# A second MLP in pairs of token blocks, with its weights reloaded for each pair and the output weights kept

## The chip, the cores and the metric

The kernel runs on one core of one Trainium2 chip. The metric is the time of one execution on the device in microseconds (us). Engines are named as the profile names them: PE multiplies matrices, PEld loads its stationary operand, DVE and ACT do elementwise work, SP issues DMA transfers. SBUF is the on-chip working memory, PSUM the accumulators that PE writes.

## The reference, cut to what matters

Attention in chunks of 64 tokens gives x, 4608 tokens by 512. Two MLPs follow; the second is the one that changes:

```python
def _moe_ref(x, w_in, w_out):               # d_ff = 2048
    h = x @ w_in
    g = np.maximum(h, 0.0) + np.log1p(np.exp(-np.abs(h)))
    return g @ w_out

def _moe2_ref(x, w1, w2, w3, w_out):        # d_model 512, d_ff = 768
    h = np.maximum(np.maximum(x @ w1, x @ w2), x @ w3)
    return h @ w_out
```

## The kernel before

Tokens go in nine blocks of 512 (`TB`). A value is carried as two float32r halves, a high and a low one, and a product is three matmuls (`PASS`: high by high, high by low, low by high). `cut_up` makes the halves: a cast (`copy_op`, ACT or DVE) and a subtraction (`tt_op`, DVE).

All work is first written down as operations for a planner (`Plan`). Each has the engines it may run on with a cost, its dependencies, the buffers it takes (`alloc`), a due time, and for transfers a landing time (`lat`, `move`). `Plan.order` walks through planned time and gives each engine the ready operation with the earliest due time whose buffers are free; the program is then written in that order, so the order on each engine, SP's queue included, and the place of each buffer are fixed before the run. PE's operations of the second MLP follow one another in the order written (`in_line("h", ...)`).

The large buffers are 46 slots of SBUF, each 128 partitions x 2 x 512 words (512 KB): kinds "w" (32), "x" (8), "z" (4), "qh" and "vh" (one each). Smaller ones are 13 tiles of 128 x 512 (kinds `LATE`) and three `g`. PSUM has two `ph` banks, two `acc` pairs of banks, and two banks `one` (X and Z), which hold sums that DVE adds up.

The second MLP multiplies by Strassen's scheme in Winograd's form: with both matrices in quarters, seven products (`SEVEN`, p1 to p7) in place of eight. Here the halves of X in the token direction are the two halves of one block, so `split` cuts a block into seven combinations (B11, T1 to T4, B21, B22), each one slot, and a product is 2 x 3 matmuls of 128 x 128 by 256 columns. The weights w1, w2, w3 are combined and cut once by `weights2` into nine units of 3 slots and a quarter tile shared by two units, which fill the "w" slots and stay for all nine blocks. A `Unit` is one block by one unit of weights: p1, p6, p2, p7 of the new unit are interleaved with p5, p4, p3 of the old one (`mlp2`). ACT copies products out of `ph` (`keep`), DVE adds those in `one` (`add`) and takes the maximum over w1, w2, w3. After every third unit two 128-row pieces of h are cut into `g`. `mlp2_out` is the output step: 12 matmuls of 512 columns with one 512 KB tile of w_out, loaded for that step from the cut copy in DRAM (`wo2d`) into one of two slots.

Before all that, attention and the first MLP run; `early` cuts w_out of the second MLP and converts w1 to w3 beside them, and the weights of the second MLP are cut as slots of the first one's weights come free.

The lines of the profile: 836 are the matmuls of a product, 954 those of an output step, 666 and 686 those of the first MLP, 254 and 256 the copies and casts, 261 DVE's combinations of two tensors, 939 the load of a w_out tile, 781 the load of X, 968 the store of the output.

Of the kernel before, what the change touches and what calls it, by code (L numbers as in the profile page):

```python
# [10 lines left out]
F32 = mybir.dt.float32  # L11
# [167 lines left out]
def tile_kernel(ctx: ExitStack, tc: tile.TileContext, q, k, v, w_in, w_out, w1, w2, w3, wo2, out):  # L179
# [22 lines left out]
    def mem(kind, n, shape, dt, where=pool):  # L202
# [14 lines left out]
        "pair": list(range(2)),  # L217
        "g": mem("g", 3, [P, 2, TB], F32R),
# [12 lines left out]
    w2d = [dram.tile([P, TB], F32, name=f"w2d{n}") for n in range(3 * NJ2)]  # L231
    x2d = [dram.tile([P, KD, TB], F32, name=f"x2d{b}") for b in range(NB)]

    names = [0]

    def slot(*kinds, shape=[P, 2, TB], dt=F32R):
        def fresh(i):
            names[0] += 1
            return pool.tile(shape, dt, tag=f"s{i}", name=f"s{i}_{names[0]}")

        return Buf(*kinds, fresh=fresh)
# [488 lines left out]
    LATE = ("tmp", "rq", "rk", "rv", "p")  # L730

# [14 lines left out]

    def weights2(n):
# [3 lines left out]
        pair = Buf("pair")  # L751
        for h, z in enumerate((a, b)):
            o = op(
                {"S": 0.48},
                lambda e, h=h, z=z: nc.sync.dma_start(out=z.t, in_=w2d[2 * n + h]),
                w=[z],
                alloc=[] if h else [a, b, c, d, pair, *ws[:3 if n % 2 else 4]],
                after=[store["w", 2 * n + h], *begun],
                lat=2.0,
                move=1.1,  # L760
            )
# [11 lines left out]
        return cut_up(ws[3], lambda: d.t[:, L], [d], cols=cols, key=n % 2, hold=[pair])  # L773

    def split(b, after):
        names = ("B11", "T1", "T2", "B21", "T3", "T4", "B22")
        raw = [slot("x", "z", dt=F32) for _ in range(2)]
# [16 lines left out]
        def make(name, one, two):  # L794
            view, t = src[name]
            z = x2[b, name] = slot("x", "z")
            tt_op(view, src[one][0], src[two][0], ALU.subtract, [src[one][1], src[two][1]], [t], alloc=[t, z])

        def put(name):
            made = (b, name) in x2  # L800
            z = x2[b, name] if made else slot("x", "z")
# [17 lines left out]

    clock = [T1]  # L820
# [6 lines left out]
    def product(b, n, p, dst, first, **kw):  # L827

        at, col, name = SEVEN[p]
        ws, x = wbuf["b", n][at], x2[b, name]  # L830
        col += HT * (n % 2) if at == 3 else 0
# [13 lines left out]
        return pe2(0.67, fn, r=parts_of(ws, n % 2 if at == 3 else "") + [x], **kw)  # L845

    class Unit:


        def __init__(u, b, n):  # L850
            u.b, u.n = b, n
            u.jp, u.i = divmod(n, 3)
            u.Y = Buf("ph")
            if u.i == 0:
# [16 lines left out]
        def y(u, p, **kw):  # L871
            return product(u.b, u.n, p, lambda: u.Y.t[:, :HT], p == 1, w=[u.Y], **kw)
# [22 lines left out]
        def p2(u):  # L895
            product(u.b, u.n, 2, lambda: two("X"), True, w=[(XZ, "X")], alloc=first_of(XZ))
            u.add(u.c[0], 0, "X")

        def p5(u):
            product(u.b, u.n, 5, lambda: two("Z"), True, w=[(XZ, "Z")])  # L900
# [5 lines left out]
        def p3(u):  # L906
            product(u.b, u.n, 3, lambda: two("Z"), False, w=[(XZ, "Z")])
# [3 lines left out]
            if u.i == 2:  # L911
                for f in range(2):
                    g = second[u.b, 2 * u.jp + f] = Buf("g")
                    cut_up(g, lambda f=f: u.m[f].t, [u.m[f]], alloc=[g])

# [11 lines left out]
    def two(key):  # L927
        return XZ.t["XZ".index(key)][:, :HT]
# [3 lines left out]

    def mlp2_out(b, j):
        g, wo = second[b, j], slot("qh", "vh")
        in_line(
            "wo2",
            op(
                {"S": 0.48},
                lambda e: nc.sync.dma_start(out=wo.t.bitcast(F32), in_=wo2d[j]),
                w=[wo],  # L940
                alloc=[wo],
# [3 lines left out]
            ),  # L945
        )
# [26 lines left out]
    def mlp2():  # L973

        units = [(b, n) for b in range(NB) for n in range(3 * NJ2 // 2)]
        old, outs = None, []
        for b, n in units + [(NB, 0)]:
            new = None
            if b < NB:
                new = Unit(b, n)  # L980
# [14 lines left out]
            if len(outs) > (b == NB - 1):  # L995
                mlp2_out(*outs.pop(0))
            if old and old.i == 2:
                outs += [(old.b, 2 * old.jp), (old.b, 2 * old.jp + 1)]
# [40 lines left out]
    split(0, begun)  # L1039
# [38 lines left out]
```

## Time and profile before

| | |
|---|---|
| median of 3 runs | 1455.72 us (1455.64 to 1456.2) |
| the profiled execution, its own time | 1458.03 us |
| its span, first to last instruction | 1456.2 us |
| PE busy | 1426.7 us, 98% of the span |
| DVE busy | 785.6 us, 54% |
| ACT busy | 454.2 us, 31% |
| DMA | 147.5 MB, 101 GB/s over the span |
| second MLP | about 890 us to the end; 61.80 us a block |

How to read it: busy time of PE is modelled and overlaps in a stream, so what a matmul costs is read from the chain of waits by time, where each piece starts as the one before ends. An idle time names what ended it. A transfer's time to landing runs from its issue on SP to its last byte.

### The profile page before, as it was taken

Reading aid. Unit: us, or ns where it says so; the run is one execution under the profiler, and the core shown is the slowest. Engines: PE = TensorE matmul, PEld = TensorE weight load, DVE = VectorE, ACT = ScalarE, POOL = GpSimd, SP = SyncE. Lnnn points to the kernel's source line nnn. Section 1 sums busy time; section 2 is a strip of 40 time slices with the busy share of each in tenths; the row PEclk is TensorE's granted clock in tenths of the full one; section 3 lists DMA queues with packets and bytes.
Section 4 is the critical chain, followed back from the end, with each engine's and each line's share of the span. In section 5 each row is a group of like instructions: output and inputs, shape, how many; then the busy total and the mean of one; then the engine's idle time right before and its main releaser. Section 6 shows DMA issues by size and latency. Waiting matters only on the chain.

```text
span 1456.2 us, 25977 instructions
## 1 busy us (share of the span) xinstructions
PE 1426.7 (98%) x10642; PEld 1242.4 (85%) x10642; DVE 785.6 (54%) x1551; ACT 454.2 (31%) x885; POOL 0.7 (0%) x7
## 2 busy tenths in 40 slices
PE   5999999999999999999999999999999999999998
PEld 4788888787888888888888888999999999999997
DVE  7887862655545544445443555555454644545443
ACT  4443332223223232232322444333232322323222
POOL 0000000000000000000000000000000000000000
PEclk8999999999999999999999999999999999999999
DMA  8563345655435334352231312132222322223122
GB/s 255 154 176 92 96 106 128 155 126 128 127 70 136 93 103 122 65 139 73 77 98 45 118 55 87 45 102 88 87 73 80 110 86 75 87 73 117 49 68 87
DMA packets 229079, 147.47 MB, mean 101 GB/s; under 512 B 168032, under 2 KB 196704, under 8 KB 228960
## 3 DMA queue, kind: packets, MB, share of 16 engines
q1 hardware_dynamic: 228144, 145.03, 34.7%
q8 instruction: 83, 1.36, 0.4%
q10 hardware_dynamic: 816, 0.79, 0.2%
q14 instruction: 36, 0.29, 0.1%
HBM read 109.58 MB, written 36.18 MB: 100 GB/s over the span
## 4 chain that ended last, share of the span: by engine, by line
PE 91%; DVE 3%; SPq 2%; DMA 2%; issue 1%; ACT 1%; ACTq 0%; DVEq 0%
PE acc L686 25%; PE ph L666 25%; PE ph L836 16%; PE one L836 12%; PE acc L954 10%; PE aps L471 2%; SPq L413 2%; DMA s<-in_moe_w_out_dram 1%; PE ph L374 1%; PE acc L471 0%; PE ph L375 0%; DVE tmp L261 0%; ACT s L254 0%; DMA s<-in_moe_w_in_dram 0%; DMA pd<-s 0%
## 5 line engine op out<-in xcount | busy, mean ns | idle before, releaser
L686 PE MATMUL acc<-g,s 128*128 128x512 f32 x1728 | 419.4, 391 | 5.0 <-DVE tmp L261 2.8
L666 PE MATMUL ph<-s,s 128*128 128x512 f32 x1728 | 416.9, 391 | 0.0
L686 PEld LDWEIGHTS acc<-g,s 128*128 128x128 f32 x1728 | 321.8, 188 | 73.5 <-issue 2.9
L666 PEld LDWEIGHTS ph<-s,s 128*128 128x128 f32 x1728 | 325.7, 189 | 68.2
L836 PE MATMUL ph<-s,s 128*128 128x256 f32 x1944 | 267.8, 283 | 0.0
L836 PEld LDWEIGHTS ph<-s,s 128*128 128x128 f32 x1944 | 251.8, 192 | 4.1
L261 DVE TENSOR_TENSOR tmp<-one,tmp 128x256 f32<-128x256 f32 x241 | 101.9, 423 | 246.9 <-PE one L836 217.4
L261 DVE TENSOR_TENSOR g<-tmp,g 128x512 fp32r<-128x512 f32 x198 | 135.5, 685 | 182.0 <-ACT g L254 181.6
L676 ACT ACTIVATE tmp<-ph 128x512 f32<-128x512 f32 x144 | 86.1, 598 | 450.1 <-PE ph L666 441.5
L254 ACT COPY tmp<-ph 128x256 f32<-128x256 f32 x268 | 100.0, 373 | 347.7 <-PE ph L836 346.5
L836 PE MATMUL one<-s,s 128*128 128x256 f32 x1458 | 201.6, 283 | 0.0
L836 PEld LDWEIGHTS one<-s,s 128*128 128x128 f32 x1458 | 186.7, 192 | 0.2
L954 PE MATMUL acc<-s,g 128*128 128x512 f32 x648 | 157.1, 391 | 0.5 <-DMA s<-wo2d 0.5
L954 PEld LDWEIGHTS acc<-s,g 128*128 128x128 f32 x648 | 118.3, 188 | 23.3 <-DMA s<-wo2d 0.9
L254 ACT CAST g<-tmp 128x512 fp32r<-128x512 f32 x196 | 121.8, 622 | 17.9 <-PE acc L686 8.4
L261 DVE TENSOR_TENSOR tmp<-tmp,tmp 128x256 f32<-128x256 f32 (+1 forms) x152 | 83.2, 548 | 4.0
L254 ACT CAST s<-tmp 128x512 fp32r<-128x512 f32 (+1 forms) x101 | 60.3, 602 | 41.1 <-DVE tmp L322 27.3
L595 DVE STREAM_TRANSPOSE s<-rq 128x512 f32<-128x512 f32 x28 | 19.9, 710 | 70.9 <-PE aps L471 43.9
L303 DVE TENSOR_SCALAR tmp<-s 128x512 int32<-128x512 int32 x56 | 23.6, 422 | 55.9 <-DMA s<-in_moe_w_dram 23.7
L261 DVE TENSOR_TENSOR s<-tmp,s 128x512 fp32r<-128x512 f32 (+1 forms) x72 | 46.3, 654 | 7.5 <-ACT s L254 6.7
L497 ACT ACTIVATE p<-p,drop 128x512 f32<-128x512 f32 x28 | 20.3, 725 | 66.4 <-DVE p L261 66.4
L254 ACT COPY tmp<-acc 128x512 f32<-128x512 f32 x53 | 29.9, 590 | 30.1 <-PE acc L954 15.8
(74 smaller groups left out, 669.9 us busy)
## 6 DMA issues: line engine op xcount, KB each, us to landing
s<-wo2d SPq DMA_DIRECT2D x54, 512.0 KB, 3.3
s<-in_moe_w_out_dram SPq DMA_DIRECT2D x22, 512.0 KB, 4.2
x2d<-tmp SPq DMA_DIRECT2D x36, 256.0 KB, 2.7
s<-in_moe_w_dram SPq DMA_DIRECT2D x18, 512.0 KB, 3.8
s<-x2d SPq DMA_DIRECT2D x18, 512.0 KB, 4.7
s<-in_moe_w_in_dram SPq DMA_DIRECT2D x16, 512.0 KB, 5.2
out_dram<-tmp SPq DMA_DIRECT2D x29, 256.0 KB, 4.5
pd<-s SPq DMA_DIRECT2D x28, 256.0 KB, 2.3
```

Source lines behind the costliest of these rows:

```text
L254: nc.scalar.copy(dst(), src())
L261: return op({"D": 0.69 * n}, lambda e: nc.vector.tensor_tensor(dst(), a(), b(), f), r=r, w=w, **kw)
L303: lambda e: nc.vector.tensor_scalar(ai(), hw(), 0x7FFFFFFF, None, ALU.bitwise_and),
L413: dma(out=dst().rearrange("p (g i) -> p g i", i=32)[a * 32:(a + 1) * 32, o // 32:(o + n) // 32, :], in_=src[b, t % HP * 2 + h, s:s + n, ha ...
L471: nc.tensor.matmul(dst[ROWS[k], r], w[ROWS[r]], x[ROWS[r]], start=True, stop=True)
L497: op({"A": 0.62}, lambda e: nc.scalar.activation(pbuf.t, pbuf.t, AF.Softplus, bias=drop[:, :1], scale=SCALE), w=[pbuf])
L595: op({"D": 0.69}, lambda e: nc.vector.transpose(qT(), Rq.t), r=[Rq], w=[(QK, "q")], alloc=[QK])
L666: nc.tensor.matmul(ph.t, w[:, wi, kk * P:(kk + 1) * P], x[kk].t[:, xi], start=(kk == 0 and wi == 0 and xi == 0), stop=(kk == KD - 1 and wi ...
L676: in_line("y", op({"A": 0.6}, lambda e: nc.scalar.activation(l.t, ph.t, AF.Softplus), r=[ph], w=[l], alloc=[l]))
L686: nc.tensor.matmul(acc[m // 2].t[:, m % 2], w[:, wi, m * P:(m + 1) * P], g.t[:, gi, :], start=(first and wi == 0 and gi == 0), stop=(last ...
L836: nc.tensor.matmul(dst(), ws.t[:, wi, col + kk * P:col + (kk + 1) * P], x.t[:, xi, kk * HT:(kk + 1) * HT], start=(first and kk == 0 and wi ...
L954: nc.tensor.matmul(acc[t // 2].t[:, t % 2], g.t[:, gi, t * P:(t + 1) * P], wo.t[:, wi], start=(j == 0 and wi == 0 and gi == 0), stop=(j == ...
```

## The change

Blocks are taken in pairs. The two halves of X in the token direction are now the two blocks of a pair, so each of the seven combinations is two slots of 512 columns (`split2`, 14 tiles, limited to 14 by the kind "xt"), and a product is 2 x 3 matmuls of 128 x 128 by 512 columns that fill a bank (`Unit2`). Four pairs go this way; the ninth block is left alone and goes through the old `Unit` and `split`.

X of a pair takes 14 slots and 6 for raw data, so the weights no longer fit beside it. Only unit 0 stays (`STAY = 1`). Units 1 to 8 are cut for the first pair as before, stored to DRAM (`w2c`, `w2e`), and read back for each later pair and for the ninth block (`again`). The kinds "ring" (3) and "ring1" (4) hold down how many units have weights in slots: three in the later pairs, up to seven in the first pair and the ninth block. Kinds "w" and "x" serve both purposes.

The six tiles of w_out are loaded once, into "qh", "vh" and "z", and stay. The h pieces of a pair's second block wait, in slots if need be, until the first block's output is done; up to two output steps follow one unit.

```diff
+        "ring": list(range(3)),
+        "ring1": list(range(4)),
+        "xt": list(range(14)),
...
+    STAY = 1
...
     def weights2(n):
-        ws = [slot("w") for _ in range(3)] + [wbuf["b", n - 1][3] if n % 2 else slot("w")]
+        ws = [slot("w", "x") for _ in range(3)] + [wbuf["b", n - 1][3] if n % 2 else slot("w", "x")]
...
+        ring = [Buf("ring", "ring1")] if n >= STAY else []
...
+        for k in range(3) if n >= STAY else ():
+            store["c", n, k] = op(
+                {"S": 0.48},
+                lambda e, k=k: nc.sync.dma_start(out=w2c[n][k], in_=ws[k].t.bitcast(F32)),
+                r=[ws[k]],
...
+        if n >= STAY and (n % 2 or n == 3 * NJ2 // 2 - 1):
+            w = slice(0, TB if n % 2 else HT)
+            store["e", n // 2] = op(
...
+    def again(n, *more):
+
+        if n < STAY:
+            return wbuf["b", n], []
+        ring = Buf("ring", *more)
+        ws = [slot("w", "x") for _ in range(3)] + [slot("w", "x") if n % 2 == 0 else wbuf["b", n - 1][3]]
+        new = ws[:3 if n % 2 else 4]
+        wbuf["b", n] = ws
+        for k, z in enumerate(new):
...
+                alloc=[] if k else [ring, *new],
+                after=[store["e", n // 2] if k == 3 else store["c", n, k]],
...
+        return ws, [ring]
...
+    def split2(two, after):
+
+        make = lambda: [slot("x", "w", dt=F32) for _ in range(2)]
+        R = make(), make()
+        T = make()
...
+        def put(name, v):
+            x2[two, name] = [slot("x", "w") for _ in range(2)]
+            held[two, name] = [Buf("xt") for _ in range(2)]
+            for kk, z in enumerate(x2[two, name]):
+                cut_up(z, lambda kk=kk: v[0][kk].t[:, v[1]], [(v[0][kk], v[1])], alloc=[z, held[two, name][kk]])
...
+    class Unit2:
...
+            u.ws, u.ring = (first_ws[n], rings[n]) if b[0] == 0 else again(n)
...
+                    for wi, xi in PASS:
+                        nc.tensor.matmul(
+                            dst(),
+                            ws.t[:, wi, col + kk * P:col + (kk + 1) * P],
+                            x[kk].t[:, xi],
...
+            return pe2(1.36, fn, r=[ws, *x], hold=u.ring + held[u.b, name], **kw)
...
     def mlp2_out(b, j):
-        g, wo = second[b, j], slot("qh", "vh")
-        in_line(
-            "wo2",
+        g = second[b, j]
+        if j not in wo2_of:
+            z = wo2_of[j] = slot("qh", "vh", "z")
             op(
...
     def mlp2():
 
-        units = [(b, n) for b in range(NB) for n in range(3 * NJ2 // 2)]
-        old, outs = None, []
-        for b, n in units + [(NB, 0)]:
+        groups = [(b, b + 1) for b in range(0, NB - 1, 2)] + [(NB - 1,)]
+        units = [(i, n) for i in range(len(groups)) for n in range(3 * NJ2 // 2)]
+        old, outs, side = None, [], []
+        for i, n in units + [(None, 0)]:
...
+                new = Unit2(groups[i], n) if i + 1 < len(groups) else Unit(NB - 1, n)
                 begin = new.p1()
-                if n == 1 and b + 1 < NB:
-                    split(b + 1, ready + [begin])
+                if n == 4 and i + 1 < len(groups):
...
-            if len(outs) > (b == NB - 1):
-                mlp2_out(*outs.pop(0))
+            for _ in range(2 if len(outs) > 3 else 1):
+                if len(outs) > (i is None or i + 1 == len(groups)):
+                    mlp2_out(*outs.pop(0))
```

The order of the instructions on PE is the same in both kernels up to the first product of the second MLP. From there on, in the regular part, it changes as follows. Rows of one kind that follow each other stand as one with a count; `ph` and `one` are the PSUM banks, `s` slots (the weights first, then X), `g` a piece of h, `acc` the output sums. Before, on PE, one unit's seven products and an output step:

```order
L836 MATMUL ph_89<-s_216_7276,s_237_7622 128x256 x6
L836 MATMUL one_7871<-s_217_7278,s_235_7546 128x256 x6
L836 MATMUL ph_90<-s_222_7343,s_235_7546 128x256 x6
L836 MATMUL ph_89<-s_220_7301,s_239_7624 128x256 x6
L836 MATMUL one_7871<-s_219_7299,s_233_7494 128x256 x6
L836 MATMUL one_7870<-s_218_7296,s_237_7622 128x256 x6
L836 MATMUL ph_89<-s_221_7323,s_239_7624 128x256 x6
L954 MATMUL acc_93<-s_214_7259,g_73 128x512 x6
L954 MATMUL acc_92<-s_214_7259,g_73 128x512 x6
```

After, on PE at the same kind of place, the last four products of such a row and the output step:

```order
L1042 MATMUL one_7917<-s_240_7597,s_262_8010 128x512 x3
L1042 MATMUL one_7917<-s_241_7602,s_262_8010 128x512 x3
L1042 MATMUL one_7916<-s_230_7480,s_263_8109 128x512 x3
L1042 MATMUL one_7916<-s_231_7499,s_263_8109 128x512 x3
L1042 MATMUL ph_90<-s_234_7537,s_265_8111 128x512 x3
L1042 MATMUL ph_90<-s_236_7558,s_265_8111 128x512 x3
L1148 MATMUL acc_93<-s_219_7299,g_72 128x512 x6
L1148 MATMUL acc_92<-s_219_7299,g_72 128x512 x6
```

A product has become two rows of three matmuls, one for each X tile, with twice the columns; the sequence of p1 to p7 and its interleaving of two units is the same. In all, 1512 matmuls of 512 columns and 378 of 256 stand where 3402 of 256 stood.

On SP, before, the last blocks' transfers are w_out tiles, X loads and output stores:

```order
L939 DMA s_372_12526<-wo2d_101 128x1024
L939 DMA s_373_12645<-wo2d_96 128x1024
L939 DMA s_374_12814<-wo2d_97 128x1024
L968 DMA out_dram<-tmp_83 128x512
L968 DMA out_dram<-tmp_82 128x512
L968 DMA out_dram<-tmp_81 128x512
L968 DMA out_dram<-tmp_80 128x512
L939 DMA s_375_12887<-wo2d_98 128x1024
```

After, on SP at the ninth block, the weights of its units come back (`w2c_0` to `w2c_2` are the three tiles of a unit, `w2e` the shared quarter tiles):

```order
L816 DMA s_447_10724<-w2c_0_123 128x1024
L816 DMA s_449_10726<-w2c_2_125 128x1024
L816 DMA s_448_10725<-w2c_1_124 128x1024
L816 DMA s_450_10798<-w2c_0_126 128x1024
L816 DMA s_454_10825<-w2c_0_129 128x1024
L816 DMA s_452_10800<-w2c_2_128 128x1024
L816 DMA s_451_10799<-w2c_1_127 128x1024
L816 DMA s_453_10801<-w2e_148 128x1024
L816 DMA s_457_10847<-w2c_0_132 128x1024
```

No w_out load is left there, and these nine are the first of 24 reloads that follow each other with no other transfer between them.

## Rows read from the trace of the kernel before

**Rows 1.** The page: span, PE's busy share, and the chain that ended last.

```profile
span 1456.2 us, 25977 instructions
PE 1426.7 (98%) x10642; PEld 1242.4 (85%) x10642; DVE 785.6 (54%) x1551; ACT 454.2 (31%) x885; POOL 0.7 (0%) x7
PE 91%; DVE 3%; SPq 2%; DMA 2%; issue 1%; ACT 1%; ACTq 0%; DVEq 0%
```

**Rows 2.** Busy time by stretch: first and last of seven regular blocks; columns as headed.

```profile
core 0: us, PE busy (x) PEld busy (x) DVE busy (x) ACT busy (x) POOL busy (x), PEclk, DMA share, GB/s
938.47:1000.27 61.80, 61.80 (x452) 58.86 (x451) 30.88 (x65) 19.00 (x45) 0.00 (x0) 1.00 0.26 86
...
1309.27:1371.07 61.80, 61.80 (x452) 58.85 (x451) 30.88 (x65) 19.00 (x45) 0.00 (x0) 1.00 0.26 86
```

**Rows 3.** The page's groups of matmuls: products and output steps.

```profile
L836 PE MATMUL ph<-s,s 128*128 128x256 f32 x1944 | 267.8, 283 | 0.0
...
L836 PE MATMUL one<-s,s 128*128 128x256 f32 x1458 | 201.6, 283 | 0.0
...
L954 PE MATMUL acc<-s,g 128*128 128x512 f32 x648 | 157.1, 391 | 0.5 <-DMA s<-wo2d 0.5
```

**Rows 4.** The chain by time (start, us, what): first MLP, then second MLP.

```profile
502.75 2.72 PE ph L666 x12
...
942.65 1.44 PE ph L836 x12
...
946.25 2.75 PE acc L954 x12
949.00 0.71 PE ph L836 x6
```

**Rows 5.** The end of the kernel: the chain by time, and DVE's last operation.

```profile
1442.94 2.76 PE acc L954 x12
...
1445.72 3.17 DMA s<-wo2d
...
1448.93 3.04 PE acc L954 x12
...
1444.89 0.69 DVE L261 TENSOR_TENSOR g<-tmp,g 128x512 fp32r<-128x512 f32 x1 [0.16 <-ACT g L254]
```

**Rows 6.** Transfers (KB each, us to landing), and the issue of a w_out load, ns.

```profile
s<-wo2d SPq DMA_DIRECT2D x54, 512.0 KB, 3.3
...
L939 SPq DMA_DIRECT2D s<-wo2d x24: 319/320/326, 1209.0 to 1445.7; - x24
```

**Rows 7.** DVE and ACT in one regular block, by form (count, busy, mean ns, idle).

```profile
L261 DVE TENSOR_TENSOR tmp<-one,tmp 128x256 f32<-128x256 f32 x27 | 11.4, 423 | 27.5 <-PE one L836 23.3 <-ACT tmp L254 4.2
L254 ACT COPY tmp<-ph 128x256 f32<-128x256 f32 x30 | 11.2, 373 | 39.2 <-PE ph L836 39.0
L261 DVE TENSOR_TENSOR tmp<-tmp,tmp 128x512 f32<-128x512 f32 x6 | 4.1, 691 | 0.2
L261 DVE TENSOR_TENSOR g<-tmp,g 128x512 fp32r<-128x512 f32 x6 | 4.1, 687 | 0.9 <-ACT g L254 0.9
L254 ACT CAST g<-tmp 128x512 fp32r<-128x512 f32 x6 | 3.7, 623 | 0.0
...
L261 DVE TENSOR_TENSOR tmp<-tmp,tmp 128x256 f32<-128x256 f32 x6 | 2.6, 425 | 0.2
L261 DVE TENSOR_TENSOR tmp<-ph,tmp 128x256 f32<-128x256 f32 x6 | 2.5, 417 | 0.0
...
L254 ACT COPY tmp<-acc 128x512 f32<-128x512 f32 x2 | 1.2, 586 | 1.8 <-PE acc L954 1.1 <-DVE tmp L256 0.7
```

**Rows 8.** Busy time by stretch again, columns as in rows 2: three stretches with dense transfers.

```profile
5.00:12.00 7.00, 4.87 (x99) 3.76 (x100) 6.43 (x14) 2.21 (x4) 0.00 (x0) 1.00 1.09 365
84.00:92.00 8.00, 8.00 (x37) 6.64 (x36) 8.00 (x18) 3.70 (x7) 0.00 (x0) 1.00 0.70 161
800.00:808.00 8.00, 8.00 (x37) 6.64 (x36) 2.33 (x4) 2.90 (x6) 0.00 (x0) 1.00 0.60 223
```

More of the change, by code (lines that the diff above doesn't have):

```diff
@@ L756, in weights2 @@
                 w=[z],
-                alloc=[] if h else [a, b, c, d, pair, *ws[:3 if n % 2 else 4]],
+                alloc=[] if h else [a, b, c, d, pair, *ring, *ws[:3 if n % 2 else 4]],
                 after=[store["w", 2 * n + h], *begun],
@@ L800, in put @@
             made = (b, name) in x2
-            z = x2[b, name] if made else slot("x", "z")
+            z = x2[b, name] if made else slot("x", "w")
             x2[b, name] = z
@@ L818, in split, with sub @@
         put("B22")
+    held = {}
+    def split2(two, after):
+        make = lambda: [slot("x", "w", dt=F32) for _ in range(2)]
+        R = make(), make()
+        T = make()
+        for h in range(2):
+            for kk in range(2):
+                for n, b in enumerate(two):
+                    op(
+                        {"S": 0.48},
+                        lambda e, h=h, kk=kk, n=n, b=b: nc.sync.dma_start(out=R[h][kk].t[:, n], in_=x2d[b][:, 2 * h + kk, :]),
+                        w=[(R[h][kk], n)],
+                        alloc=[] if n else [R[h][kk]],
+                        after=[store[b, 2 * h + kk]] + after,
+                        lat=2.0,
+                        move=1.1,
+                    )
+        def sub(z, a, b, alloc=False):
+            for kk in range(2):
+                view = lambda v, kk=kk: v[0][kk].t[:, v[1]]
+                tt_op(
+                    lambda view=view: view(z),
+                    lambda view=view: view(a),
+                    lambda view=view: view(b),
+                    ALU.subtract,
+                    [(a[0][kk], a[1]), (b[0][kk], b[1])],
+                    [(z[0][kk], z[1])],
+                    alloc=[z[0][kk]] if alloc else [],
+                )
+        def put(name, v):
[3 more added lines that the diff above has]
+                cut_up(z, lambda kk=kk: v[0][kk].t[:, v[1]], [(v[0][kk], v[1])], alloc=[z, held[two, name][kk]])
+        r11, r12, r21, r22, t1, t2 = (R[0], 0), (R[0], 1), (R[1], 0), (R[1], 1), (T, 0), (T, 1)
+        put("B11", r11)
+        sub(t1, r12, r11, True)
+        sub(t2, r22, t1)
+        put("T2", t2)
+        put("B21", r21)
+        sub(r12, r22, r12)
+        put("T3", r12)
+        put("T1", t1)
+        sub(r21, r21, t2)
+        put("T4", r21)
+        put("B22", r22)
     clock = [T1]
@@ L825, in pe2, with product @@
         return o
-    def product(b, n, p, dst, first, **kw):
+    def product(u, p, dst, first, **kw):
         at, col, name = SEVEN[p]
-        ws, x = wbuf["b", n][at], x2[b, name]
-        col += HT * (n % 2) if at == 3 else 0
+        ws, x = u.ws[at], x2[u.b, name]
+        col += HT * (u.n % 2) if at == 3 else 0
         def fn(e):
@@ L843, in fn @@
                     )
-        return pe2(0.67, fn, r=parts_of(ws, n % 2 if at == 3 else "") + [x], **kw)
+        return pe2(0.67, fn, r=[ws, x], hold=u.ring, **kw)
     class Unit:
@@ L853, in __init__ @@
             u.Y = Buf("ph")
+            u.ws, u.ring = again(n, "ring1")
             if u.i == 0:
@@ L906, in p3 @@
         def p3(u):
-            product(u.b, u.n, 3, lambda: two("Z"), False, w=[(XZ, "Z")])
+            product(u, 3, lambda: two("Z"), False, w=[(XZ, "Z")])
             u.add(u.c[0], 1, "Z")
```

135 lines of the change are left out of this document (114 added, 21 removed).

## The prediction

> **What bounds the kernel now.** I read the page first, then the stage table, then the chain of waits by time, then the operation groups. PE is busy for 98% of the span, and 91% of the chain that ended last is PE work [rows 1]. The chain's share is what counts: nearly every microsecond of the second MLP is a matmul waiting for the matmul before it. The stage table shows the regular part: each 512-token block of the second MLP takes 61.80 us, the same in the first regular block and in the last one, with PE busy throughout at a granted clock of 1.00, DVE busy 30.9 us, ACT 19.0 us and DMA a quarter [rows 2]. So only two things can shorten this stage: fewer or cheaper matmuls, or the removal of the one wait that shows, at the very end [rows 5]. The reader is to see in the page's groups that the second MLP's products (L836) are 1944 + 1458 = 3402 matmuls of 256 columns, 9 blocks of 378, and its output steps (L954) 648 matmuls of 512 columns [rows 3]. The mean durations there (283 and 391 ns) overlap their neighbours and are not prices. The price of a matmul in a stream is read from the chain by time, where each ends after the one before.
>
> **The products.** Twelve 256-column products in a row take 1.44 us, which is 120.0 ns each; twelve 512-column matmuls of the first MLP (L666), which read the same kind of slot and write a whole bank, take 2.72 us, 226.7 ns each [rows 4]. Two 256-column matmuls cost 240.0, one of 512 costs 226.7, so each pair that becomes one saves 13.3 ns. The change turns 8 of the 9 blocks into 4 pairs: 8 x 378 = 3024 small matmuls become 4 x 378 = 1512 wide ones; the ninth block keeps its 378 small ones. The order shows it: a product is now two runs of three 512-column matmuls where it was one run of six with 256. Saving: 1512 x 13.3 ns = **20.2 us**, all on the chain, since PE is the chain. The bound from the other side is the nearest 512-column row in this stage, the output steps: 2.75 us for twelve, 229.2 ns each [rows 4]. With that the saving is 1512 x 10.8 = 16.4 us. I take 226.7: the 2.75 stands beside a neighbour of 0.71 where half of its peers' 1.44 is 0.72, so part of the excess is only where the profile draws the border. If the excess is a price of changing between widths, most of the 48 output steps of the pairs lose it: a gain of at most 48 x 0.02 = 1.0 us more. I count it at nothing and keep it for the range.
>
> Beside it a rule speaks against so large a gain. The Trainium skill, "TensorE: Matmul & The Clock Gate", section Back-to-back issue gap, gives the gap of warm matmuls as the columns at 2.4 GHz plus 2.5 ns, so that width would hardly matter; the estimate by that page is 1512 x about 2.5 ns = 3.8 us instead of 20.2. The trace does not agree: at a granted clock of 1.00 [rows 2] the two rows, 120.0 and 226.7 ns, differ by 106.7 ns for 256 columns, and what is left over in each is 13.3 ns, not 2.5 [rows 4].
>
> **The w_out tiles.** Before, every output step loads its 512 KB tile again, 54 loads through two slots [rows 6]. After, six tiles are loaded once and stay. In the regular part these loads cost nothing (no wait for them stands in any regular block), so there is no gain there. At the end there is one: PE ends a step at 1445.70, waits 3.17 us for a w_out tile, and starts the last step at 1448.93 [rows 5]. The last operand from DVE was finished at 1444.89 + 0.69 = 1445.58, before PE came free at 1445.70, so nothing else is late behind the wait: **3.2 us** go. What follows (3.04 us of matmuls, the copy, the last stores) stays.
>
> **DVE and ACT.** The pair's work is re-cut, not enlarged. Before, one block costs DVE 39 operations of 256 columns (27 + 6 + 6, at 0.42 us) and 23 of 512 (6 + 6 and 11 for cutting X, at 0.69), 32.3 us, which is the stage table's 30.9 with the overlap [rows 2, 7]. After, a pair costs 51 combinations of 512 columns, 12 second halves of g and 24 operations for X: 87 x 0.69 = 60.0 us in a pair of about 118 us, where two blocks cost 64.6 in 123.6. The share stays at one half. ACT goes from 30 copies at 0.373 and 13 casts at 0.622 a block (19.3 us) to 30 copies at about 0.59 (the copy of 512 columns out of an accumulator) and 26 casts a pair: 33.9 us in 118 [rows 7]. A bank must be read within two products before PE needs it again; two products last 2.72 us now and lasted 1.44, and one operation of 512 columns takes 0.69, so the handover becomes looser. I cost all this at nothing. Its cover is the half of the time in which DVE is idle. Where it is thinnest is the change of pair, since the 14 X tiles of the next pair take the places of the old ones only as their last products end: 14 x 0.69 = 9.7 us of DVE inside some 20 us of PE work, beside the units' own work. If a quarter of that showed at each of the 3 changes it would cost 7 us; I keep 0 to 7 us for the range.
>
> **The reloads.** New work: in pairs 2 to 4 and for the ninth block, units 1 to 8 read their cut weights back, 3 tiles each and 4 more for the shared quarter tiles, one of them half: 27.5 loads of 512 KB, four times; and once the same is stored. Each costs SP about 0.32 us to issue and lands 3.3 us later when alone [rows 6]. 27.5 x 0.52 MB = 14.4 MB in a pair of 118 us is 122 GB/s, less the 54-load traffic that goes. The trace sustains 365 GB/s where the queue is kept full [rows 8]. Three sets are open: one finishing, one running, one loading; a set is freed in the middle of the next unit and refilled for a unit that begins about 15 us later, against 3.3 us and three more transfers at 1.44 us (0.52 MB at 365 GB/s), 7.6 us. So I cost the reloads at nothing in the pairs. SP's queue is in order: the reloads stand before the output stores and the X loads, whose consumers come a whole unit later. In the first pair, where weights are still cut by DVE, the 28.5 stores wait in SP for DVE; behind them stand loads of raw weights for units several places later, up to seven sets open.
>
> **The ninth block** is the tight place: its units of 42 x 120.0 ns = 5.04 us need 27.5 / 8 = 3.4 loads each, 4.9 us at 365 GB/s. What keeps it covered are the 14 output steps that the order puts into this stretch (14 x 2.72 = 38 us) and the reloads running up to seven sets ahead, as the order shows: 24 in a row on SP without a store between them.
>
> **Sum.** The profiled execution took 1458.0 us, 1456.2 of it span [rows 1]. 1458.0 - 20.2 - 3.2 = 1434.6 for a profiled execution; the median of the runs, 1455.7, lies 2.3 below it, so the forecast is **1432.3 us**.
>
> **Rivals.**
> *The ninth block waits for its weights.* For it: mixed stretches moved only 223 GB/s (800 to 808 us) and 161 (84 to 92) [rows 8]. At 223 a load takes 2.35 us and a unit's share 8.1 us, 3.0 more than a unit without output steps; two of the nine have none and four have two, so some 6 us stay: 1438. At 161 the 27.5 loads would take 90 us, more than the stage's own 83 us: some 1447. Against: a queue kept full held 365 for seven microseconds, and these reloads stand 24 in a row.
> *Columns, not matmuls, carry the cost.* If the wide products took twice 120.0 ns, only the 3.2 us would remain: 1455.7 - 3.2 = 1452.5. Against it stands the 226.7 of the first MLP. The page of the Trainium skill named above, TensorE: Matmul & The Clock Gate, would put it between, at an estimate of 1448.7.
> *Slower: the ring comes too late.* Place: the first product of each of the 32 reloaded units. If a set were freed a unit later than I think (its hold lasts until the last product of the unit, which runs inside the next), the landing would show, at least 3.3 us x 32 = 106 us: 1538. It decides from 23.4 / 32 = 0.73 us for each unit. For it: before, no weight moved at all in this stage, and nothing in the trace shows such a reload. Against: DMA busy only a quarter there [rows 2], and the 15 us against 7.6.
> *The change doesn't do what it says* is excluded by the order: 1512 wide and 378 small products stand in it.
>
> **How the numbers follow.** Forecast 0.77 (1430 to 1436: from 1.0 and 1.3 us below for the output steps and the runs' own spread, to 3.8 above for 229.2 ns); small waits at the changes of pair 0.05 (1434 to 1440); ninth block 0.10 (1436 to 1441); columns 0.03; ring 0.05. The range 1429.5 to 1440 holds the first two and most of the third, about 0.88, and is no wider than these bounds. A measurement here tells 0.2%, 2.9 us, from no change. Faster: all but the ring and half of the columns, 0.93; within 0.2%: 0.02; slower: 0.05.
>
> **What would show it.** Right: twelve 512-column products in 2.72 us in the chain by time, a pair in about 118.3 us (378 x 0.2267 + 12 x 2.72), no idle of PE before the pair's products (line 1042 of the changed kernel), the last step starting as the one before ends, DVE near one half. Wrong: "DMA s<-w2c" or "s<-w2e" in the chain (ring, or ninth block by its place), DVE or ACT as releaser of PE at the change of pair, or 2.88 us for twelve wide products (columns).

## The result, and the profile after

The changed kernel takes **1433.43 us** (median of 4 runs, 1432.72 to 1436.79) where the kernel before took 1455.96 beside it (4 runs, 1455.64 to 1457.31). The ratio is **0.9848**, 95% interval 0.9831 to 0.9865: 22 us less, between 19.7 and 24.6. The forecast was 1432.3 in a range of 1429.5 to 1440. The whole comes out right and one of its two terms does not, as the runs below show.

The page of the kernel after, against [rows 1] and [rows 3]: its span, the engines' busy time, the chain that ended last by engine, and the matmul groups of the second MLP. Products of the pairs are now line 1042, those of the ninth block line 942 (not in the table's largest groups), output steps line 1148.

```profile
span 1430.9 us, 22911 instructions
...
PE 1406.5 (98%) x9130; PEld 1164.8 (81%) x9130; DVE 769.3 (54%) x1400; ACT 437.3 (31%) x760; POOL 0.7 (0%) x7
...
PE 94%; SPq 2%; DMA 2%; DVE 1%; issue 1%; ACT 1%; ACTq 0%; DVEq 0%
...
L1042 PE MATMUL ph<-s,s 128*128 128x512 f32 x864 | 212.3, 389 | 0.0
...
L1042 PE MATMUL one<-s,s 128*128 128x512 f32 x648 | 158.8, 389 | 0.0
...
L1148 PE MATMUL acc<-s,g 128*128 128x512 f32 x324 | 77.6, 390 | 0.0
L1148 PE MATMUL acc<-s,s 128*128 128x512 f32 x324 | 77.3, 389 | 0.0
```

There are 864 + 648 = 1512 wide products, as forecast, and the idle time before every one of these groups is 0.0. The 0.5 us that stood before the output steps in [rows 3] is gone. PE is still the chain.

The chain by time (start us, us, what), first in a pair, then at the end of the kernel:

```profile
1010.89 2.72 PE ph L1042 x12
1013.61 2.72 PE one L1042 x12
1016.33 1.36 PE ph L1042 x6
1017.69 5.44 PE acc L1148 x24
...
1413.28 2.75 PE acc L1148 x12
1416.03 0.71 PE one L942 x6
1416.74 0.72 PE ph L942 x6
1417.46 0.85 PE one L942 x6
1418.31 8.20 PE acc L1148 x36
```

Twelve wide products take 2.72 us, 226.7 ns each, the price that the prediction took from the first MLP. Twenty-four output matmuls between them take 5.44, also 226.7 each; in the ninth block, between products of 256 columns, twelve take 2.75 again. At the end, the last three output steps run as one piece of 36: the wait of [rows 5] is gone.

Busy time by stretch (columns as in [rows 2]): one pair from a place in it to the same place in the next, then the first two stretches of 20 us behind the ninth block's first product, which starts at 1338.48.

```profile
1121.05:1239.37 118.32, 118.32 (x523) 97.99 (x523) 57.87 (x91) 34.03 (x59) 0.00 (x0) 1.00 0.43 158
...
1340.00:1360.00 20.00, 20.00 (x134) 18.43 (x133) 9.33 (x18) 5.74 (x13) 0.00 (x0) 1.00 1.02 402
1360.00:1380.00 20.00, 20.00 (x126) 18.09 (x126) 5.58 (x12) 3.28 (x8) 0.00 (x0) 1.00 0.30 105
```

A pair takes 118.32 us (forecast 118.3), against 2 x 61.80 of two blocks in [rows 2]; DVE is busy 57.87 us of it (forecast 60.0) and ACT 34.03 (33.9), PE the whole. From 1340 to 1360, while the ninth block's weights come back, the DMA engines are full, share 1.02 and 402 GB/s, more than the 365 that the prediction had seen in [rows 8], and PE is busy in every one of those microseconds.

For all that follows, **the stage** is the time from the first product of the second MLP to the end of the last matmul, both from the chain by time. What comes before it is the same work on PE in both kernels.

| kernel | first product, us | last matmul ends, us | stage, us |
|---|---|---|---|
| before | 889.36 | 1451.97 | 562.61 |
| after | 885.77 | 1426.51 | 540.74 |

The stage is 21.87 us shorter. Its pieces of the chain, added up by line: products 407.83 before (3402 matmuls, 119.9 ns each), 388.17 after (1512 at 226.7 and 378 at 120.1), 19.7 less; output steps 229.6 ns for each matmul before and 227.1 after, 1.6 less over 648; and 0.5 of a wait at the end. (The front ended 3.6 us earlier in this one execution; the last experiment shows that it moves by as much from run to run.)

### The profile page after: what moved, and what is told of

The parts are those of the page before. It is cut to its first block, busy times and chain, and to the rows that moved or that the text cites. A ratio compares the mean times of both kernels' runs of the same rounds, so it can differ in the third digit from the quotient of the medians.

```text
span 1430.9 us, 22911 instructions
## 1 busy us (share of the span) xinstructions
PE 1406.5 (98%) x9130; PEld 1164.8 (81%) x9130; DVE 769.3 (54%) x1400; ACT 437.3 (31%) x760; POOL 0.7 (0%) x7
## 4 chain that ended last, share of the span: by engine, by line
PE 94%; SPq 2%; DMA 2%; DVE 1%; issue 1%; ACT 1%; ACTq 0%; DVEq 0%
PE acc L691 26%; PE ph L671 26%; PE ph L1042 14%; PE acc L1148 10%; PE one L1042 10%; PE aps L476 2%; PE ph L942 2%; PE one L942 1%; SPq L418 1%; PE acc L476 1%; PE ph L379 1%; DMA s<-in_moe_w_out_dram 1%; ACT s L259 1%; PE ph L380 0%; DMA s<-in_k_dram 0%
## 5 line engine op out<-in xcount | busy, mean ns | idle before, releaser
L671 PE MATMUL ph<-s,s 128*128 128x512 f32 x1728 | 416.8, 391 | 0.1
L671 PEld LDWEIGHTS ph<-s,s 128*128 128x128 f32 x1728 | 325.6, 189 | 68.2 <-DVE s L266 0.2
L1042 PE MATMUL ph<-s,s 128*128 128x512 f32 x864 | 212.3, 389 | 0.0
L266 DVE TENSOR_TENSOR tmp<-one,tmp 128x512 f32<-128x512 f32 (+1 forms) x125 | 79.1, 633 | 213.8 <-PE one L1042 175.4
L1042 PEld LDWEIGHTS ph<-s,s 128*128 128x128 f32 x864 | 162.2, 188 | 33.6
L259 ACT COPY tmp<-ph 128x512 f32<-128x512 f32 (+1 forms) x140 | 75.8, 542 | 278.4 <-PE ph L1042 218.1
L1042 PE MATMUL one<-s,s 128*128 128x512 f32 x648 | 158.8, 389 | 0.0
L1042 PEld LDWEIGHTS one<-s,s 128*128 128x128 f32 x648 | 121.5, 188 | 25.1
L1148 PE MATMUL acc<-s,g 128*128 128x512 f32 x324 | 77.6, 390 | 0.0
L1148 PE MATMUL acc<-s,s 128*128 128x512 f32 x324 | 77.3, 389 | 0.0
L1148 PEld LDWEIGHTS acc<-s,s 128*128 128x128 f32 x324 | 60.6, 188 | 12.5
L266 DVE TENSOR_TENSOR tmp<-tmp,tmp 128x512 f32<-128x512 f32 (+1 forms) x112 | 69.4, 621 | 2.4
```

Source lines behind the costliest of these rows:

```text
L259: nc.scalar.copy(dst(), src())
L266: return op({"D": 0.69 * n}, lambda e: nc.vector.tensor_tensor(dst(), a(), b(), f), r=r, w=w, **kw)
L671: nc.tensor.matmul(ph.t, w[:, wi, kk * P:(kk + 1) * P], x[kk].t[:, xi], start=(kk == 0 and wi == 0 and xi == 0), stop=(kk == KD - 1 and wi ...
L1042: nc.tensor.matmul(dst(), ws.t[:, wi, col + kk * P:col + (kk + 1) * P], x[kk].t[:, xi], start=(first and kk == 0 and wi == 0 and xi == 0), ...
L1148: nc.tensor.matmul(acc[t // 2].t[:, t % 2], g.t[:, gi, t * P:(t + 1) * P], wo.t[:, wi], start=(j == 0 and wi == 0 and gi == 0), stop=(j == ...
```

## The experiments

In the edited kernels the lines shift a little: products of the pairs are 1042 or 1044, output steps 1148 or 1149. Line 1134 is the load of a w_out tile, 816 the reload of weights, 886 the load of X for a pair, 259 a copy on ACT.

### Width alone

**e1_halves** keeps the whole change, pairs, reloads, resident w_out, and splits each wide product matmul back into two of 256 columns.

```diff
-                for kk in range(2):
-                    for wi, xi in PASS:
-                        nc.tensor.matmul(
-                            dst(),
...
-                            x[kk].t[:, xi],
-                            start=(first and kk == 0 and wi == 0 and xi == 0),
+                for c in range(2):
+                    part = slice(c * TB // 2, (c + 1) * TB // 2)
+                    for kk in range(2):
+                        for wi, xi in PASS:
+                            nc.tensor.matmul(
+                                dst()[:, part],
...
+                                x[kk].t[:, xi, part],
+                                start=(first and c == 0 and kk == 0 and wi == 0 and xi == 0),
...
```

> The changed kernel with each 512-column product matmul of the pairs split into two of 256 columns; reloads, resident w_out, DVE and ACT work stay. Theory (a matmul carries a fixed 13.3 ns beside its columns): 3024 matmuls of 120.0 ns instead of 1512 of 226.7, so 20.2 us longer: about 1453.6 us against 1433.4. The stretch from the first product to the last matmul, 540.7 us in the changed kernel, becomes about 561. Rival (the gain comes from the fewer and longer DVE and ACT operations or from the resident w_out, not from the width): stays within 3 us of 1433.4. The page TensorE: Matmul & The Clock Gate of the Trainium skill would give an estimate of 3.8 us longer.

Measured: 1456.22 us (10 runs), ratio to before 0.9998 (0.9989 to 1.0008); stage 561.46, which is 20.72 longer than after's, as expected. The median is 2.6 above the expected 1453.6; in the one execution with a profile the first product starts at 889.12, 3.35 later than in after's, so that the excess lies ahead of the stage. Its chain by time, near the place shown above of after:

```profile
1017.59 1.43 PE ph L1044 x12
1019.02 1.44 PE one L1044 x12
1020.46 2.88 PE ph L1044 x24
```

120.0 ns each, exactly [rows 4]. So nearly all of the gain hangs on the width of the product matmuls: pairs, the ring and the resident tiles with narrow products give no gain that the medians can tell. (Twice the columns also means half as many matmuls and half as many weight loads; no run parts these.) The stage is 1.15 us shorter than before's; 0.53 of that is the wait at the end. Most of the rest lies in the output steps: added up matmul by matmul in PE's trace, with the waits left out, they take 148.6 us before, 147.8 here and 147.1 after. So half of what they gain is there without the width, and the other half came with it. Here and in the kernel after they stand in 36 runs between products, before in 52; whether that brings the first half is not shown.

**e2_quarters** goes one step on, four matmuls of 128 columns (`range(4)` and `TB // 4` in the same edit), to ask whether 13.3 ns is a fixed price for each matmul whatever its width.

> The same with four matmuls of 128 columns: a third width for the price law. Theory (13.3 ns fixed plus 0.4167 ns a column, from 120.0 and 226.7): 66.7 ns each, 6048 of them 403 us instead of 343, so about 1494 us. Rival (each matmul loads its own weights, and that load sets a floor near the 120 ns seen at 256 columns): 6048 x 120 = 726 us, so about 1816 us. In between means a floor between 66.7 and 120 ns.

Measured: 1769.97 us (one run), stage 875.14. The chain by time:

```profile
1014.92 5.36 PE one L1044 x48
1020.28 5.36 PE ph L1044 x48
```

5.36 / 48 = 111.7 ns each, not the 66.7 of a straight line through 120.0 and 226.7. Halving the columns from 256 to 128 saves 8 ns instead of 53. The line through 256 and 512 columns does not reach down to 128. It looks like a floor near 111 ns, lower than the 120 of the rival, but no narrower width was run. The Trainium skill, "TensorE: Matmul & The Clock Gate", section LDWEIGHTS, gives the time of a weight load as its columns at 1.2 GHz; by that the estimate for the 128 columns that each matmul here loads is 106.7 ns, and the 111.7 is 5 ns above it. It fits, but no run here changed the weight load, so that cause is not shown. The Trainium skill's section Back-to-back issue gap, on the same page, does not fit: its sustained 81 ns for 128 columns and 131 for 512 stand against 111.7 and 226.7.

### The w_out tiles

**e4_before_wo_ahead** puts the one gain that the prediction saw in w_out, 3.2 us, into the kernel before: in the last block the six tiles get slots of their own, those that X no longer needs, and so arrive early.

```diff
-        g, wo = second[b, j], slot("qh", "vh")
+        g, wo = second[b, j], slot("qh", "vh", "z") if b == NB - 1 else slot("qh", "vh")
```

> The kernel before, with four more slots for the w_out tiles of the last block alone, so that they are loaded ahead: the resident w_out's effect at the end, alone. Theory (0.5 us of idle PE): the stretch from the first product to the last matmul shrinks from 562.6 to about 562.1 us; the time is the same within its noise, 1455.4. Rival (3.2 us, as predicted): 559.4 us, and 1452.8.

Measured: 1455.61 us (10 runs), ratio 0.9994 (0.9983 to 1.0005); stage 561.78, 0.83 shorter than before's. PE has no wait left in the stage, and what went with it is far from 3.2 us. Why, PE's timeline of the kernel before shows (start us, us, engine, line, operation, count, and in brackets the idle time ahead of it and what ended it):

```profile
1442.78 5.63 PE L954 MATMUL acc<-s,g 128*128 128x512 f32 x24
1448.93 3.02 PE L954 MATMUL acc<-s,g 128*128 128x512 f32 x12 [0.53 <-DMA s<-wo2d]
```

From 1442.78 PE ran two steps, 24 matmuls, and not one; it was idle for 0.53 us. The chain of [rows 5] follows the load back to its issue at 1445.72 and leaves out the second of the two steps, which ran beside the transfer. The page's row had the right number all along, 0.5 us in [rows 3].

**e3_wo_again** takes the resident tiles out of the kernel after: w_out is loaded again for each output step, as before.

```diff
-        if j not in wo2_of:
-            z = wo2_of[j] = slot("qh", "vh", "z")
+        wo = slot("qh", "vh")
+        in_line(
+            "wo2",
...
-                lambda e: nc.sync.dma_start(out=z.t.bitcast(F32), in_=wo2d[j]),
+                lambda e: nc.sync.dma_start(out=wo.t.bitcast(F32), in_=wo2d[j]),
...
```

> The changed kernel with w_out loaded again for every output step through two slots, as before the change; all else stays. Theory (the wait at the end of the kernel before was only 0.5 us of idle PE, the rest of the 3.17 us on the chain lay beside an output step): 0.5 us longer at the end, 1434. Some 2 to 3 us more are possible in the ninth block, where these loads now queue behind the reloads on SP; they would show there as PE waiting for a w_out tile. Rival (the wait was worth 3.2 us at the end, as predicted): 1436.6, with 3.2 us of idle PE before the last step.

Measured: 1442.61 us (4 runs), ratio 0.9909 (0.9894 to 0.9924); stage 547.93, 7.2 longer than after's, when 0.5 was expected and 3.5 at most. PE's waits in the stage (engine, line, for what: us in total, times, longest):

```profile
PE ph L1042 <- ACT tmp L259: 3.0, 2, 2.2
PE acc L1149 <- DMA s<-wo2d: 2.7, 3, 1.4
```

Only 0.5 of this is the wait at the end; the 1.5 of the 7.2 that are no wait lie in the matmuls right behind the five waits. ACT, the other releaser, was itself held (its timeline, then the waits of SP's queue in the stage, here and in the kernel before):

```profile
1063.44 0.59 ACT L259 COPY tmp<-ph 128x512 f32<-128x512 f32 x1 [6.33 <-DMA out_dram<-tmp]
```

```profile
SPq L1134 <- PE acc L1149: 334.7, 51, 19.9
...
SPq L939 <- PE acc L954: 490.1, 52, 17.7
```

SP stood 334.7 us before w_out loads whose slot PE had not yet left. In such a time nothing behind goes out: not the output stores, whose `tmp` ACT needs for its next copy, and not the reloads. The kernel before has the same wait, 490.1 us of it in the stage, and PE waited there for nothing but the 0.53 us at the end; it had no reloads to stand behind. Both waits for ACT stand in the sixth of a pair's nine units, in pairs 2 and 3, soon after SP has loaded X for the next pair. In the ninth block it goes the other way round, the reloads stand ahead of w_out (busy time by stretch, columns as above):

```profile
1370.00:1380.00 10.00, 9.13 (x61) 8.24 (x60) 3.93 (x8) 2.15 (x5) 0.00 (x0) 1.00 1.02 414
1380.00:1390.00 10.00, 8.61 (x56) 7.56 (x55) 0.85 (x2) 1.12 (x3) 0.00 (x0) 1.00 0.49 168
```

That this is the queue's order and not the transfers was so far a reading. **e8_wo_pool** tests it: e3_wo_again with the w_out loads issued from GpSimd's queue, which has nothing else to do there. PE's order stays.

```diff
-                {"S": 0.48},
-                lambda e: nc.sync.dma_start(out=wo.t.bitcast(F32), in_=wo2d[j]),
+                {"G": 0.48},
+                lambda e: nc.gpsimd.dma_start(out=wo.t.bitcast(F32), in_=wo2d[j]),
```

> The kernel with w_out loaded again for each output step (e3_wo_again), with one thing changed: those 54 loads are issued from GpSimd's queue, which is otherwise empty there, and no longer from SP's. PE's order of work is the same. Theory (SP's queue is in order, so a w_out load that waits for its slot holds the stores and reloads behind it, and the prefetched reloads hold the w_out loads): the second MLP's waits of PE for ACT (3.0 us) and those for w_out in the ninth block (2.2 us) vanish; only the wait before the last step, about 0.5 us, may stay. The stage (first product of the second MLP to the last matmul's end) takes 540.7 to 541.5 us and not 547.9; the median about 1434 to 1436 us. Rival (the transfers themselves: the w_out loads take the DMA engines' time from the reloads, or come late by their own 3 to 9 us of landing): the stage stays at 545 to 548 us, median 1440 to 1443.

Measured: 1436.03 us (4 runs), ratio 0.9863 (0.9847 to 0.988); stage 542.32. The same bytes move, and 5.6 of the 7.2 us are back; the stage is 0.8 above the top of what the theory gave. GpSimd's waits, then PE's timeline at the only wait that PE has left in the stage:

```profile
POOL s L1134 <- PE acc L1149: 603.3, 52, 146.5
```

```profile
1420.04 5.63 PE L1149 MATMUL acc<-s,g 128*128 128x512 f32 x24
1426.92 3.01 PE L1149 MATMUL acc<-s,g 128*128 128x512 f32 x12 [1.25 <-DMA s<-wo2d]
```

GpSimd waits 603.3 us for the slots and PE loses nothing by it; no other transfer of the stage is issued there. The waits for ACT and those inside the ninth block are gone, as the theory said; the last one is 1.25 us and not 0.5, since that load goes out 0.4 us later than from SP and takes 3.52 us from issue to landing where [rows 5] has 3.17. What e8_wo_pool does not part is a load that is issued late and one that lands late behind reloads issued before it: in e3_wo_again the w_out load that ended the 1.39 us wait in the ninth block went out at 1373.20, once SP had issued the reloads ahead of it, and then took 9.34 us to land. The Trainium skill has the place of the wait for GpSimd's path: by "DMA: Bandwidth & Descriptors", section Anatomy of one DMA — SWDGE (gpsimd) path, DMA engines do not wait on semaphores, the issuing sequencer does, before it dispatches. GpSimd's 603.3 us agree, and so do the 334.7 of SP's queue.

### The ring and the ninth block

**e5_ring2** gives the ring of the reloads two sets instead of three (`"ring": list(range(2))`); the borrowed slots of `ring1`, by which sets run further ahead, stay.

> The changed kernel with two sets of reloaded weights open in the later pairs instead of three (six instead of seven in the first pair and the ninth block): the ring brought one step nearer to the rival that it comes too late. A unit's reload can then start only when the last product of the unit before it has run, some 4 us of products and one or two output steps (2.7 to 5.4 us) before its own first product. Theory (a reload takes 3.3 us for its first tile and 1.4 for each more, and the tiles are needed one after another over the unit): just enough, no PE wait, 1433 to 1435 us, stage 540.7 to 542. Rival (the ring is near its edge): 24 units wait 1 to 3 us each, 1457 to 1505.

Measured: 1433.84 us (4 runs), ratio 0.9851 (0.9835 to 0.9868); stage 540.73 and no wait of PE in it. One set fewer costs nothing, so the rival (24 units wait) falls.

**e7_two_sets** takes the borrowed slots too, so that the reloads of the ninth block can run one unit ahead and not seven.

```diff
-        "ring": list(range(3)),
+        "ring": list(range(2)),
...
-            u.ws, u.ring = again(n, "ring1")
+            u.ws, u.ring = again(n)
```

> As the run with two sets, and two sets in the ninth block too (before: six). There the units last 5.04 us without an output step, and a unit's 3.4 reloads take 4.9 us at 365 GB/s. Theory (the sets loaded ahead are what covers the ninth block): 3 to 10 us of PE waiting for w2c or w2e tiles in the last 90 us, none in the pairs; 1436 to 1444. Rival (transfers are far from the bound there): stage 540.7, no waits, 1433.4.

Measured: 1435.2 us (4 runs, 1434.56 to 1436.61), ratio 0.9859 (0.9845 to 0.9874); stage 540.74, no wait of PE. The expected 3 to 10 us do not show. The stretches of the table above, in this kernel:

```profile
1340.00:1360.00 20.00, 20.00 (x129) 18.22 (x128) 8.40 (x16) 5.79 (x13) 0.00 (x0) 1.00 0.09 36
1360.00:1380.00 20.00, 20.00 (x126) 18.09 (x125) 6.09 (x13) 3.13 (x8) 0.00 (x0) 1.00 0.74 280
```

The same transfers lie later, 36 and 280 GB/s where after has 402 and 105, and still in time. Of the two covers that the prediction named for the ninth block, the reloads far ahead are not needed, as long as no w_out load stands in SP's queue; the other, the output steps between its products, is still there and was not tested.

**e9_both_small** takes that last condition away: w_out again through SP (e3_wo_again) and two sets (e7_two_sets) together.

> The kernel with w_out loaded again for each output step (e3_wo_again), with the shorter ring for the reloads (two sets and no borrowed slots, as in e7_two_sets). What it tells apart: whether the wait of the ninth block comes from the 24 reloads that stand ahead of the w_out loads on SP. Theory: with two sets hardly any stand ahead, so the 2.2 us of waits for w_out in the ninth block vanish, while PE's waits for ACT at the start of pairs (3.0 us), where w_out loads hold the stores, stay: stage about 545 to 546 us, median about 1438 to 1440. Rival (the w_out loads wait for their own slots, whatever stands ahead): no change from e3_wo_again, stage 547 to 548.5 us; or, if now the reloads come late behind waiting w_out loads, longer, up to 555 us.

Measured: 1456.23 us (10 runs), ratio 0.9998 (0.9986 to 1.001); stage 566.91, 26.2 longer than after's. Alone the one costs 7.2 us and the other nothing; together they eat the whole gain. Neither expectation reached that far. PE's waits in the stage:

```profile
PE ph L942 <- DMA s<-w2c: 8.2, 5, 3.0
PE ph L1042 <- DMA s<-w2c: 7.2, 3, 3.1
PE ph L942 <- ACT tmp L259: 0.5, 1, 0.5
PE acc L1149 <- DMA s<-wo2d: 0.5, 1, 0.5
```

The theory was right that the w_out waits of the ninth block go (0.5 is the end's), and wrong that the pairs keep their waits for ACT. Now a w_out load that waits stands ahead of a reload that is needed at once. In the pairs this is not at their start, where the expectation had put the waits for ACT: all three waits stand in the sixth of nine units, in pairs 2, 3 and 4. SP's timeline ahead of the first of them:

```profile
1040.22 1.30 SPq L886 DMA_DIRECT2D s<-x2d  x2
1049.72 0.32 SPq L1134 DMA_DIRECT2D s<-wo2d  x1
...
1052.44 0.32 SPq L1134 DMA_DIRECT2D s<-wo2d  x1
1052.81 0.91 SPq L816 DMA_DIRECT2D s<-w2c  x2
```

For 8 us, up to 1049.72, nothing goes out, since a w_out load waits for its slot; the reload that PE needs goes out at 1052.81, behind the next w_out load. The other five waits for reloads are in the ninth block.

All waits together are 16.4 us. In the other 9.8 PE waits for nothing. Where such time goes the matmuls right after a wait show (PE's timeline, then busy time by stretch, columns as above):

```profile
1059.26 2.90 PE L1042 MATMUL ph<-s,s 128*128 128x512 f32 x6 [2.77 <-DMA s<-w2c]
...
1182.31 2.90 PE L1042 MATMUL ph<-s,s 128*128 128x512 f32 x6 [3.06 <-DMA s<-w2c]
...
1305.20 1.61 PE L1042 MATMUL ph<-s,s 128*128 128x512 f32 x6 [1.40 <-DMA s<-w2c]
...
1411.31 0.95 PE L942 MATMUL ph<-s,s 128*128 128x256 f32 x6 [2.32 <-DMA s<-w2c]
...
1415.95 0.95 PE L942 MATMUL ph<-s,s 128*128 128x256 f32 x6 [2.26 <-DMA s<-w2c]
```

```profile
1059.26:1062.15 2.89, 2.89 (x7) 2.31 (x8) 0.36 (x1) 0.00 (x0) 0.00 (x0) 0.50 1.05 408
...
1064.00:1066.00 2.00, 2.00 (x11) 1.64 (x10) 1.90 (x4) 0.00 (x0) 0.00 (x0) 1.00 1.00 399
1182.31:1185.21 2.90, 2.90 (x7) 2.32 (x8) 0.07 (x1) 0.00 (x0) 0.00 (x0) 0.50 1.05 410
...
1305.20:1308.00 2.80, 2.79 (x12) 2.34 (x13) 0.00 (x0) 0.59 (x1) 0.00 (x0) 1.00 0.96 345
...
1411.31:1413.60 2.29, 2.29 (x18) 2.18 (x18) 0.48 (x2) 0.37 (x1) 0.00 (x0) 1.00 0.98 381
...
1417.30:1420.50 3.20, 3.20 (x17) 3.20 (x17) 1.54 (x3) 0.06 (x2) 0.00 (x0) 0.50 1.03 421
```

After 2.77 us without work the granted clock is 0.50, the lower of the two levels (1.2 GHz), and six wide matmuls take 2.90 us, more than twice their usual 1.36; soon after it is 1.00 again. After 3.06 it is the same; after 1.40 it stays at 1.00, and the six take 1.61. It stays at 1.00 after 2.32 us too, and is at 0.50 soon after the next wait, of 2.26; so the length of one wait alone does not tell what follows. The wait of 2.96 us that ends at 1433.44 is followed by 0.50 as well. Set against the same matmuls of the kernel after, all of the 9.8 us lies in the matmuls right behind the ten waits: 1.7, 3.2, 1.7 and 1.7 us behind the four that the half clock followed (2.77, 3.06, 2.26 and 2.96), and 0.2 to 0.3 behind each of the other six.

### The front

**after_again** is the kernel after once more, unchanged, to ask whether the 3.6 us by which its front ended earlier belong to the change.

> The changed kernel once more, for the spread of the part before the second MLP: its profiled execution began the second MLP 3.6 us earlier than the kernel before did, though nothing of the change lies there. Theory (spread from run to run): the first product starts at 887 to 890 us and the stage from it takes 540.7 us again. Rival (the change shortens the first part): it starts at 886 or earlier again.

Measured: 1435.75 us (4 runs, 1431.97 to 1439.31), ratio 0.9861 (0.9839 to 0.9884). First product at 892.36 and not 885.77, later than either expectation; stage 540.74 again. The front spreads by more than 6 us from run to run of one kernel; the stage is the same to 0.01. So kernels are compared here by the stage first, and medians that differ by 2 us are not told apart.

## Why the prediction was right, and where it was not

**The products: right.** 20.2 us were forecast from two rows of the chain. The pieces of the chain give 19.7; the experiment that undoes the width alone gives 20.72, with what the output steps gain by it. The choice of 226.7 over 229.2 ns was right: the 2.75 of [rows 4] belongs to steps that stand between narrow products. Between wide ones it is 2.72, and in the ninth block, where products are still narrow, 2.75. The reason given, that part of the excess is only the profile's border, is not shown: 20.72 is 0.6 more than the product rows account for, so some of it is a price. The 1.0 us allowed for this as a bound holds for what the width does to the output steps (0.7 us, e1_halves). In all they gained about 1.6 by the chain, since as much again came without the width; that part the prediction did not see.

**The w_out tiles: the step that failed.** The term was 3.2 us and measured 0.53. The prediction said that PE "waits 3.17 us for a w_out tile", from a piece of the chain of waits. It had looked whether DVE's operand was late, but not whether PE was at work meanwhile; the chain shows one path, and where a transfer lies on it the engine may be running another step. The engine's own row with its idle time was in [rows 3]. The missing 2.7 us were made up by the output steps, by about 1.6, which the forecast had at nothing; the stage came out 21.87 us shorter where 23.4 were forecast. That the median then lies only 1.1 above the forecast is in part luck: the front alone spreads by more than that.

There is a second error in the same term, which no number of the forecast shows. The prediction weighed the tiles by their own waits alone and said that in the regular part there is "no gain there". With the reloads in SP's queue these loads are not harmless any more: they cost 7.2 us with the ring as it is and 26.2 with a shorter one. That the tiles are resident is not a gain of 3 us against the kernel before; it keeps SP's queue free of waiting loads, and that is what lets the reloads cost nothing.

**DVE and ACT: right.** 57.87 and 34.03 us in a pair were 60.0 and 33.9, and no wait stands at a change of pair. The 0 to 7 us kept for it were not needed.

**The reloads and the ninth block: right in the result.** Nothing shows, and the rival at 1438 to 1447 falls: the mixed stretches' 223 and 161 GB/s [rows 8] were no limit of the queues, which moved 402 here. One of the two reasons given, that reloads run far ahead, is not needed (e7_two_sets); the other, the output steps in that stretch, stands untested. The rival of the late ring (1538) falls for this kernel. Its mechanism is real, though: e9_both_small shows it at 8 places where PE waits for a reload, at some 2 us each and with half the clock behind four of them, once SP's queue holds them up.

**Columns against matmuls: the rival falls**, at 20.72 us for the width alone, and with it the 3.8 us that the prediction had worked out as an estimate from the 2.5 ns of the Trainium skill, "TensorE: Matmul & The Clock Gate", section Back-to-back issue gap, where it is the figure of an isolated matmul. The left-over of 13.3 ns for each matmul is the measured one at 256 and at 512 columns, not at 128.

## What to carry to other kernels

Price a matmul from a run of them in the chain by time, at the width and among the neighbours that it will have; a price at two widths is no line to a third. A transfer on the chain is a wait only as far as the engine's own row shows idle time beside it. Before you put transfers with a deadline on a queue, look for loads in it that wait for a slot: a wait that was free before holds everything behind it. Moving such loads to an idle queue, or not needing them, can be worth more than a deeper ring: with two sets, doing without the w_out loads is worth 26.2 us (e9_both_small against e7_two_sets), and the deeper ring with these loads in place 19.0 (against e3_wo_again).

## What the runs showed of the hardware

- With each matmul loading its own 128 columns of weights, one takes 226.7 ns at 512 columns, 120.0 at 256 and 111.7 at 128: at a granted clock of 1.00, 13.3 ns over the columns' time at 2.4 GHz for the first two, and 58 ns over it for the third.
- One core's transfers ran at 402 GB/s over 20 us with the DMA share at 1.02 and PE busy throughout, and at 399 to 421 in stretches of 2 to 10 us at shares of 1.00 to 1.05, most of them beside waits of PE.
- Idle times of 2.77 and 3.06 us on PE were each followed by matmuls at a granted clock of 0.50, six of which took 2.90 us in place of 1.36; after 1.40 us, and after one idle time of 2.32, the clock stayed at 1.00. A pause costs more than its length: 0.2 to 0.3 us more where the clock stayed up, 1.7 to 3.2 where it fell.
